# Cross attention with states and a maxout FFN on one core: when three state matrices are transposed and placed, and when x is loaded

## The chip, the core and the metric

The kernel runs on one core of one Trainium2 chip. The metric is the device time of one execution in microseconds (us). Five engines work beside each other and meet through semaphores: TensorE (PE in the profile; its weight loads are PEld), VectorE (DVE), ScalarE (ACT), GpSimd (POOL) and SyncE (SP). SP only issues DMAs here. DMAs issued by GpSimd run on queue 0 of the profile ("software"), those of SP on queue 1, those of ACT on queue 10 (both "hardware"); all of them use the same 16 DMA engines.

## What is computed

There are 8 batches b of 8 heads h. x[b, h] is 512 x 64, state[b, h] is 32 x 64. The weights are 512 x 768 (three) and 768 x 512.

```
scores = x @ state.T / 8                 # 512 x 32 per head
a      = softmax(scores)
xread  = a @ state                       # 512 x 64
a2     = softmax(state @ x.T / 8)        # 32 x 512
sread  = a2 @ x                          # 32 x 64
t      = concat([xread, sread], axis=2)  # 544 rows per head; heads side by side: 8*544 x 512
h      = max(t @ w1, t @ w2, t @ w3)     # x 768
out    = h @ w_out                       # 4352 x 512, float32
```

## The kernel before

All matmuls are in bf16. The kernel never forms xread: it multiplies each head's state with the weights once a batch (G = state @ W, by `g_piece`, `g_cols`) and then multiplies the softmax a with G (`x_maxout`). So for each batch b it needs

- `xT[b]`, x transposed. Batches 0 to 2 transpose on TensorE (`x_transpose`), batches 3 to 7 by a DMA from SP (`x_transpose_dma`, L196), into three buffers in turn;
- `bds[k]` for the pair of batches 2k and 2k+1: the transposed states of each pair of heads as a block diagonal, zero elsewhere. It is made in four steps: `load_st(k)` loads `st_f[k]` (128 KB), `states_cast(k)` makes a bf16 copy `st[k]`, twice side by side (L136), `states_transpose(k)` transposes it into `stT[k]`, on TensorE into PSUM or by a DMA from SP (L154, L158), and `states_place(k)` copies the two halves of 64 partitions into the block diagonal (L163, two instructions);
- `scores(b)`: TensorE multiplies xT[b] with bds (L210), ACT takes the exponential into e (L215);
- `softmax(b)`: VectorE sums and inverts into rden (L223, L225), GpSimd multiplies e by it into a (L230, 1.91 us);
- `aT[b]`, a transposed: on TensorE for b up to 2 (`a_transpose`), by a DMA from SP after that (`a_transpose_dma`, L246);
- `x_pad(b)`: GpSimd copies x[b] into one of two buffers xp with columns of ones between the heads (L256, 1.88 us); `sread(b)` multiplies e with it on TensorE (L277), and its result goes through a small DMA transpose into `ats` (L289, `late_transposes`), read only by the last round;
- `x_maxout(b, m)` for the six column blocks m of 128: six matmuls (L383), ACT copies one product (L387), VectorE takes the two maxima (L390, L391);
- `ffn_out(b, j)` for four row blocks j: six matmuls (L421), ACT copies into `osb[b]` (L424), and at j = 2 and j = 3 GpSimd stores half a batch each (L435), 512 KB.

The order of the instructions on every engine is the order in which the program issues them; nothing is reordered. A written-out prologue handles batches 0, 1 and the front part of 2. Then a loop over b = 2 to 7 runs `x_maxout(b, m)` for m = 0 to 5 and, behind each, the functions of a list `slots[m]`: the scores, softmax, padding and transposes of batch n = b + 1, the G of both, and `ffn_out(b - 1)`. What one engine must wait for holds up all that was issued behind it on that engine. GpSimd's queue therefore mixes arithmetic (a, x_pad, states_cast, states_place) with the issue of loads and stores; SP's queue holds all DMA transposes in order.

The lines around the change, in order of issue: in the prologue `load_st(1, nc.gpsimd)` and `load_x(2)` (L470), `wout`, `load_st(2)`, `load_st(3)`, `load_x(3)`, `load_x(4)`, the memsets of xp and bds on GpSimd; then, later in the prologue, the three `states_cast`, `x_pad(2)`, and `states(1, act)`, which transposes st[1] on TensorE into a PSUM tile of the tag "two" (made by `spare`) and places it by ACT. Scores and softmax of batch 2 follow, `x_transpose_dma(3)`, the DMA transposes of st[2] and st[3], `load_x(5)`, and `states_place` of both on GpSimd. In the loop, `load_x(n + 3)` is in slot 0.

Of the kernel before, what the change touches and what calls it, by code (L numbers as in the profile page):

```python
# [8 lines left out]
F32 = mybir.dt.float32  # L9
# [6 lines left out]
def kernel(  # L16
# [40 lines left out]
    def load_st(k, eng):  # L57
        eng.dma_start(
            out=st_f[k],
            in_=state[2 * k:2 * k + 2].rearrange("b h n d -> (b h n) d").rearrange("(p t) d -> p t d", t=4))  # L60
# [8 lines left out]
    def load_x(b):  # L69
        nc.gpsimd.dma_start(  # L70
            out=x_sb[b][:, 0:XW].rearrange("p (h jd) -> p h jd", h=H),
            in_=x[b].rearrange("h (p j) d -> p h (j d)", j=J))
# [51 lines left out]
    def keep_busy(n):  # L124
        p = pp.tile([128, 1024], F32, tag="two", name="idle")
        for _ in range(n):
            nc.tensor.matmul(p[:, 0:512], zero[:, 0:128], zero, start=True, stop=True)  # L127
# [9 lines left out]

    stT = {}

    def spare(shape):  # L140
        t = pp.tile([128, 2048], BF16, tag="two", name="spare")
        n = 1
        for d in shape[1:]:
            n *= d
        t = t[:, 0:n]
        if len(shape) == 3:
            return t.rearrange("p (a b) -> p a b", a=shape[1])
        return t.rearrange("p (a b c) -> p a b c", a=shape[1], b=shape[2])

    def states_transpose(k, dma):  # L150

        if dma:
            stT[k] = data.tile([128, 4, 128], BF16, name=f"stT{k}")
            nc.sync.dma_start_transpose(out=stT[k], in_=st[k].rearrange("p t c d -> p (t c d)"))  # L154
        else:
            stT[k] = pp.tile([128, 4, 128], BF16, tag="pw", bufs=4, name="pt") if k == 0 else spare([128, 4, 128])
            for t in range(4):
                nc.tensor.transpose(stT[k][:, t, :], st[k][:, t].rearrange("p c d -> p (c d)"), ident)  # L158

    def states_place(k, copy):  # L160
        for c in range(2):
            r = slice(64 * c, 64 * c + 64)
            copy(out=bds[k][r, :, :, c, :].rearrange("p b h (q t) -> p (b h) q t", t=4),  # L163
                 in_=stT[k][r].rearrange("p t (k q) -> p k q t", q=8))

    def states(k, copy):
        states_transpose(k, False)
        states_place(k, copy)
# [7 lines left out]
    def x_transpose(b, g, *copies):  # L176

        if g == 0:
            new(xT, b, [128, H, 2, 128], "xT", bufs=3)
        n = HS // len(copies)  # L180
        for k, copy in enumerate(copies):
            if (b, g) == (2, 0):
                p = spare([128, n, 2, 128])
            else:
                p = pp.tile([128, n, 2, 128], BF16, tag="pw", bufs=4, name="pxt")
            for s in range(n):
                for jj in range(2):
                    nc.tensor.transpose(  # L188
                        p[:, s, jj, :],
                        xv[b][:, 2 * (n * k + s) + g, 2 * jj:2 * jj + 2, :].rearrange("p j d -> p (j d)"),  # L190
                        ident)
            copy(out=xT[b].rearrange("p (s g) j t -> p g s j t", g=2)[:, g, n * k:n * k + n], in_=p)  # L192

    def x_transpose_dma(b):
        new(xT, b, [128, H, 2, 128], "xT", bufs=3)
        nc.sync.dma_start_transpose(out=xT[b].rearrange("p h j t -> p (h j) t"), in_=x_sb[b][:, 0:XW])  # L196
# [131 lines left out]
    def g_cols(b, ms, copies=(act, act), defer=(False, False)):  # L328
        flush_copies()
        for m, copy, wait in zip(ms, copies, defer):  # L330
            if m == 0:
                new(G, b, [128, 2, NM * 384], "G", bufs=3)
            p = pp.tile([128, 2, 512], F32, tag="two", name="pg")
            pv = p[:, :, 0:384].rearrange("p g (i f) -> p g i f", i=3)
            for s in range(HS):
                for g in range(2):
                    nc.tensor.matmul(  # L337
                        pv[32 * s:32 * s + 32, g], bd(b, 2 * s + g)[64 * g:64 * g + 64, g, :],
                        m_cols(w_sb, m)[64 * g:64 * g + 64, s],
                        start=True, stop=True, tile_position=(64 * g, 32 * s))  # L340

            def place(m=m, pv=pv, copy=copy):
                copy(out=m_cols(G[b], m), in_=pv)  # L343

            if wait:
                copies_due.append(place)
            else:
                place()
# [54 lines left out]

    def ffn_out(b, j, split=False):
        if j == 0:
            osb[b] = work.tile([128, J, d_model], F32, tag="osb", name="osb")
        rows = None if b == "s" else out[b * SP:b * SP + S, :].rearrange("(p j) f -> p j f", j=J)
        if split:
            for k, (copy, eng) in enumerate(((dve, nc.sync), (act, nc.scalar))):
                f = slice(256 * k, 256 * k + 256)  # L410
                p = pp.tile([128, 256], F32, tag="pw", bufs=4, name="ph")
                for m in range(NM):
                    nc.tensor.matmul(p, ht[b][:, m, j * 128:(j + 1) * 128], wout_sb[:, m, f],  # L413
                                     start=(m == 0), stop=(m == NM - 1))
                oh = work.tile([128, 256], F32, tag=f"oh{k}", bufs=1, name="oh")
                copy(out=oh, in_=p)
                eng.dma_start(out=rows[:, j, f], in_=oh)
            return
        p = pp.tile([128, d_model], F32, tag="pw", bufs=4, name="po")
        for m in range(NM):  # L420
            nc.tensor.matmul(p, ht[b][:, m, j * 128:(j + 1) * 128], wout_sb[:, m, :],  # L421
                             start=(m == 0), stop=(m == NM - 1))
        o = osb[b]
        act(out=o[:, j, :], in_=p)  # L424
        if b == "s":
            for k in range(4 * j, 4 * j + 4):
                r0 = k * SP + S
                (nc.sync if k % 4 < 2 else nc.gpsimd).dma_start(
                    out=out[r0:r0 + Ns, :], in_=o[32 * (k % 4):32 * (k % 4) + 32, j, :])
            return  # L430
        if b == B - 1 and (j == 1 or j == 2):
            nc.sync.dma_start(out=rows[:, j - j % 2:j + 1, :], in_=o[:, j - j % 2:j + 1, :])
        elif b < B - 1 and j >= 2:
            j0 = 2 * j - 4
            nc.gpsimd.dma_start(out=rows[:, j0:j0 + 2, :], in_=o[:, j0:j0 + 2, :])  # L435
# [19 lines left out]
    load_w(3, (0,))  # L455
    keep_busy(2)
    x_transpose(1, 0, act)
    keep_busy(8)
    g_cols_fast(0, 0)
    a_transpose(0, 0, act)  # L460
# [6 lines left out]
    scores(1, 1, 2)  # L467
    softmax(1, 1, 2, (nc.gpsimd.tensor_mul, J))
    load_w(3, (2,))
    load_st(1, nc.gpsimd)  # L470
    load_x(2)
    nc.gpsimd.dma_start(out=wout_sb, in_=moe_w_out.rearrange("(kk p) f -> p kk f", p=128))
    for k in range(2, B // 2):
# [4 lines left out]
        nc.gpsimd.memset(t.rearrange("p (k c) -> p k c", c=PW)[:, :, 0:2], 1.0)  # L478
    for k in range(1, B // 2):
        nc.gpsimd.memset(bds[k], 0.0)  # L480
    g_cols(0, (1,))
    g_cols(1, (0,))
    sread(0)
# [10 lines left out]
    x_maxout(0, 3)  # L494
    g_cols(0, (4, 5), defer=(False, True))
    x_maxout(1, 2)
    for k in range(1, B // 2):
        states_cast(k, pool)
    x_pad(2)
    x_maxout(0, 4)  # L500
    states(1, act)
    x_transpose(2, 0, dve)
    x_maxout(0, 5)
    g_cols(1, (4, 5), defer=(False, True))
# [2 lines left out]
    scores(2, 0, 2)  # L507
    softmax(2, 0, 2, (nc.gpsimd.tensor_mul, J))
    x_transpose_dma(3)
    for k in range(2, B // 2):  # L510
        states_transpose(k, True)
    late_transposes()
    ffn_out(0, 0)
    x_maxout(1, 4)
    ffn_out(0, 1)
    load_x(5)
    sread(2)
    g_front(2)
    for k in range(2, B // 2):
        states_place(k, pool)  # L520
    x_maxout(1, 5)
    a_transpose(2, 0, act)
    a_transpose(2, 1, dve)
# [6 lines left out]
    for b in range(2, B):  # L530
        n = b + 1
        slots = [[] for _ in range(NM)]
        if n < B:
            slots[0].append(lambda: scores(n, 0, 2))
            slots[1].append(lambda: softmax(n, 0, 2, (nc.gpsimd.tensor_mul, J)))
            slots[1].append(lambda: x_pad(n))
            slots[2].append(lambda: a_transpose_dma(n))
            if n + 2 < B:
                slots[2].append(lambda: x_transpose_dma(n + 2))
            slots[5].append(late_transposes)  # L540
            if n + 3 < B:
                slots[0].append(lambda: load_x(n + 3))
        else:
            for m in range(NM):
                slots[m].append(lambda m=m: s_maxout(m))
        slots[1].append(lambda: g_back(b))
        if n < B:
            slots[4].append(lambda: sread(n))
            slots[4].append(lambda: g_front(n))
        for j, m in enumerate((1, 2, 4, 5)):  # L550
            slots[m].insert(0 if m > 2 else len(slots[m]), lambda j=j: ffn_out(b - 1, j))
        for m in range(NM):
            x_maxout(b, m)
            for f in slots[m]:
                f()
# [36 lines left out]
```

## Time and profile before

| what | value |
|---|---|
| median of 8 runs | 156.45 us (154.94 to 162.09) |
| the profiled execution's own time | 156.33 us |
| its span, first to last instruction | 154.4 us |
| mean granted TensorE clock | 0.996 |
| busy: PE, DVE, ACT, POOL | 146.4, 97.4, 94.9, 64.8 us |
| DMA: moved, mean rate over the span | 21.72 MB, 141 GB/s |

The span is what the trace covers; the execution's own time has 1.93 us more around it. Busy times are unions of an engine's instructions. A row of the page's groups names the line, the engine, the operation, what it writes and reads, and behind the bars its busy time, the mean ns of one, and the idle time of the engine just before these instructions with what ended it. A row of the timeline has start, duration, engine, line, operation and in brackets the idle time before it and what ended that.

### The profile page before, as it was taken

The page shows a single profiled execution, that of the slowest core. Times are in us where ns is not written, and L with a number is a line of the kernel's source. Part 1 is how long each engine was busy: PE and PEld are TensorE (multiplying, and loading weights), DVE is VectorE, ACT ScalarE, POOL GpSimd, SP SyncE. Part 2 cuts the span into 40 slices and gives each one's busy share as a digit, 9 for nine tenths or more (in the row PEclk, how much of TensorE's full clock was granted, in tenths as well). Part 3 has the DMA queues.
Part 4 walks back from the last instruction along what each step waited for, and adds up shares of the span by engine and source line. Part 5 has one row for each costly group of instructions (what it writes and reads, how often), then busy time and mean ns, then how long its engine had stood idle before and what let it go on. Part 6 is the DMA issues. An engine that isn't in the chain of part 4 may idle for free.

```text
span 154.4 us, 3500 instructions
## 1 busy us (share of the span) xinstructions
PE 146.4 (95%) x1390; PEld 71.7 (46%) x1390; DVE 97.4 (63%) x177; ACT 94.9 (61%) x147; POOL 64.8 (42%) x79
## 2 busy tenths in 40 slices
PE   6999999999999967999999999999999999999990
PEld 2555433554444433444444453445344556665450
DVE  3478867869538653768576857785768583565110
ACT  3667688895768446674777477656865637333340
POOL 8997899065229953055106410741073100100050
PEclk9999999999999999999999999999999999999998
DMA  4999999998997799959990883060306030110374
GB/s 110 206 183 190 196 180 162 232 201 122 122 179 134 250 169 154 190 166 235 139 216 6 164 188 136 2 202 15 136 4 204 16 133 0 66 72 0 140 239 169
DMA packets 36736, 21.72 MB, mean 141 GB/s; under 512 B 21968, under 2 KB 34384, under 8 KB 36720
## 3 DMA queue, kind: packets, MB, share of 16 engines
q0 software_dynamic: 17232, 15.08, 53.3%
q1 hardware_dynamic: 19344, 6.29, 22.9%
q8 instruction: 11, 0.18, 0.5%
q10 hardware_dynamic: 144, 0.13, 0.2%
q14 instruction: 5, 0.04, 0.1%
HBM read 15.20 MB, written 8.91 MB: 156 GB/s over the span
## 4 chain that ended last, share of the span: by engine, by line
PE 78%; DMA 9%; POOL 4%; ACT 4%; SPq 1%; issue 1%; DVE 0%
PE pw L383 39%; PE po L421 23%; DMA stT<-st 5%; PE idle L127 4%; DMA aT<-a 4%; PE pg L311 3%; POOL a L230 2%; PE ps L210 2%; ACT G L343 1%; PE pxt L188 1%; PE psr L277 1%; PE pg L337 1%; POOL bd L163 1%; PE psh L210 1%; PE ph L413 1%
## 5 line engine op out<-in xcount | busy, mean ns | idle before, releaser
L383 PE MATMUL pw<-aT,G 128*128 128x512 bf16 x288 | 69.0, 379 | 1.2 <-DMA aT<-a 0.9
L390 DVE TENSOR_TENSOR t<-t,pw 128x512 bf16<-128x512 bf16 (+1 forms) x54 | 35.1, 650 | 30.5 <-ACT t L387 30.4
L421 PE MATMUL po<-wout,ht 128*128 128x512 bf16 x198 | 47.4, 379 | 0.2 <-DVE t L390 0.2
L383 PEld LDWEIGHTS <-G 128*128 128x128 bf16 x288 | 26.7, 98 | 33.2 <-issue 2.7
L391 DVE TENSOR_TENSOR ht<-t,pw 128x512 bf16<-128x512 bf16 (+1 forms) x54 | 35.6, 658 | 5.6
L424 ACT COPY osb<-po 128x512 f32<-128x512 f32 x33 | 19.3, 585 | 29.6 <-PE po L421 29.6
L387 ACT CAST t<-pw 128x512 bf16<-128x512 f32 (+1 forms) x54 | 30.5, 566 | 10.1 <-PE pw L383 9.3
L421 PEld LDWEIGHTS <-ht 128*128 128x128 bf16 x198 | 18.8, 98 | 23.8 <-issue 2.8
L318 ACT CAST G<-pg 128x1024 bf16<-128x1024 f32 x24 | 24.5, 1022 | 3.6 <-PE pg L311 3.2
L435 POOL DMA_DIRECT2D out_dram<-osb x14 | 7.8, 561 | 44.3 <-ACT osb L424 35.7
L230 POOL TENSOR_TENSOR a<-e,rden 128x1024 bf16<-128x1024 bf16 (+2 forms) x10 | 15.2, 1527 | 23.9 <-PE pw L383 15.4
L256 POOL COPY xp<-x 128x2048 bf16<-128x2048 bf16 x6 | 11.3, 1882 | 0.0
L223 DVE TENSOR_REDUCE den<-e 128x32 f32<-128x1024 bf16 (+1 forms) x10 | 9.9, 995 | 0.8 <-ACT e L215 0.7
L343 ACT CAST G<-pg 128x768 bf16<-128x768 f32 x11 | 8.7, 811 | 1.4 <-PE pg L337 1.4
L109 POOL DMA_DIRECT2D w<-in_moe_w_dram x12 | 9.2, 783 | 0.1
L383 PE MATMUL pw<-ats,w 128*128 128x256 bf16 x72 | 8.8, 273 | 0.0
L215 ACT ACTIVATE e<-ps 128x1024 bf16<-128x1024 f32 x6 | 6.2, 1031 | 3.7 <-PE ps L210 3.7
L127 PE MATMUL idle<-zero 128*128 128x512 bf16 x20 | 7.1, 505 | 1.2 <-DVE zero L85 1.2
L383 PEld LDWEIGHTS <-w 128*128 128x128 bf16 x72 | 7.0, 98 | 2.1
L311 PE MATMUL pg<-w,bd 64*32 64x512 bf16 x192 | 7.5, 381 | 0.0
L163 POOL COPY bd<-stT 64x512 bf16<-64x512 bf16 x4 | 4.3, 1072 | 6.2 <-DMA stT<-st 6.0
L210 PEld LDWEIGHTS <-xT 128*128 128x128 bf16 x128 | 5.0, 98 | 2.2 <-ACT xT L192 0.3
(63 smaller groups left out, 87.9 us busy)
## 6 DMA issues: line engine op xcount, KB each, us to landing
out_dram<-osb POOLq DMA_DIRECT2D x14, 512.0 KB, 4.1
x<-in_x_dram POOLq DMA_DIRECT2D x6, 512.0 KB, 9.9
w<-in_moe_w_dram POOLq DMA_DIRECT2D x6, 256.0 KB, 6.2
x<-in_x_dram POOLq DMA_DIRECT2D x3, 256.0 KB, 6.0
w<-in_moe_w_dram POOLq DMA_DIRECT2D x6, 128.0 KB, 6.1
wout<-in_moe_w_out_dram POOLq DMA_DIRECT2D x1, 768.0 KB, 11.8
x0f<-in_x_dram SPq DMA_DIRECT2D x1, 512.0 KB, 3.9
out_dram<-osb SPq DMA_DIRECT2D x1, 512.0 KB, 2.6
```

The source lines that it names most:

```text
L127: nc.tensor.matmul(p[:, 0:512], zero[:, 0:128], zero, start=True, stop=True)
L230: mul(out=a[b][:, r, g0:g1].rearrange("p j g s n -> p j (g s) n"), in0=e[b][:, r, g0:g1].rearrange("p j g s n -> p j (g s) n"), in1=rden[: ...
L256: nc.gpsimd.tensor_copy(out=x_pads[b % 2][:, 2:2 + 2 * H * PW].rearrange("p (k c) -> p k c", c=PW)[:, :, 0:2 * D], in_=x_sb[b][:, 0:XW].re ...
L311: nc.tensor.matmul(ps[g][32 * s:32 * s + 32], bd(b, 2 * s + g)[64 * g:64 * g + 64, g, :], w_sb[64 * g:64 * g + 64, s, c0:c1], start=True, ...
L318: copy(out=G[b][:, :, c0:c1], in_=p[:, :, 0:n])
L343: copy(out=m_cols(G[b], m), in_=pv)
L383: nc.tensor.matmul(p[:, 0:n], lhs(i, k), rhs(k), start=(k == 0), stop=(k == nk - 1))
L387: nc.scalar.copy(out=t0[:, 0:n], in_=pw[0][:, 0:n])
L390: nc.vector.tensor_max(t1[:, 0:n], t0[:, 0:n], pw[1][:, 0:n])
L391: nc.vector.tensor_max(ht[b][:, m, :], t1[:, 0:n], pw[2][:, 0:n])
L421: nc.tensor.matmul(p, ht[b][:, m, j * 128:(j + 1) * 128], wout_sb[:, m, :], start=(m == 0), stop=(m == NM - 1))
L424: act(out=o[:, j, :], in_=p)
```

## The change

- `load_st(1)` is issued from ACT's queue after the copy of xT of batch 1, instead of from GpSimd after the weights; at its old place on GpSimd stands `states_cast(1)`, and SP transposes st[1] by a DMA then. `states_place(1)` is done by GpSimd behind the memsets of bds. The transposes on TensorE and the copies on ACT for k = 1 are gone, and with them `spare`; its second user, `x_transpose(2, 0)`, takes its PSUM tile directly.
- st[2] is still transposed ahead of the loop, st[3] in round b = 2 of the loop, behind the transpose of x[5]. `states_place(2)` and `states_place(3)` are issued in slot 3 of rounds b = 2 and 3.
- `load_x(5)` moves from ahead of the loop into slot 0 of round 2, and x[6] and x[7] follow one round later than before.
- `osb` has three buffers instead of two. The lines that store are not touched: each batch is stored in two halves before and after.

```diff
-    def spare(shape):
-        t = pp.tile([128, 2048], BF16, tag="two", name="spare")
...
-            stT[k] = pp.tile([128, 4, 128], BF16, tag="pw", bufs=4, name="pt") if k == 0 else spare([128, 4, 128])
+            stT[k] = pp.tile([128, 4, 128], BF16, tag="pw", bufs=4, name="pt")
...
-                p = spare([128, n, 2, 128])
+                p = pp.tile([128, 2 * n, 2, 128], BF16, tag="two", name="spare")[:, 0:n]
...
-            osb[b] = work.tile([128, J, d_model], F32, tag="osb", name="osb")
+            osb[b] = work.tile([128, J, d_model], F32, tag="osb", bufs=3, name="osb")
...
     x_transpose(1, 0, act)
+    load_st(1, nc.scalar)
     keep_busy(8)
...
     load_w(3, (2,))
-    load_st(1, nc.gpsimd)
+    states_cast(1, pool)
+    states_transpose(1, True)
     load_x(2)
...
     for k in range(1, B // 2):
         nc.gpsimd.memset(bds[k], 0.0)
+    states_place(1, pool)
...
-    for k in range(1, B // 2):
+    for k in range(2, B // 2):
         states_cast(k, pool)
     x_pad(2)
     x_maxout(0, 4)
-    states(1, act)
     x_transpose(2, 0, dve)
...
     x_transpose_dma(3)
-    for k in range(2, B // 2):
-        states_transpose(k, True)
+    states_transpose(2, True)
     late_transposes()
     ffn_out(0, 0)
     x_maxout(1, 4)
     ffn_out(0, 1)
-    load_x(5)
     sread(2)
     g_front(2)
-    for k in range(2, B // 2):
-        states_place(k, pool)
...
             if n + 2 < B:
                 slots[2].append(lambda: x_transpose_dma(n + 2))
+                slots[0].append(lambda: load_x(n + 2))
+            if b == 2:
+                slots[2].append(lambda: states_transpose(3, True))
             slots[5].append(late_transposes)
-            if n + 3 < B:
-                slots[0].append(lambda: load_x(n + 3))
+            if b < 4:
+                slots[3].append(lambda: states_place(b, pool))
```

More of the change, by code (lines that the diff above doesn't have):

```diff
@@ L138 @@
     stT = {}
-    def spare(shape):
-        t = pp.tile([128, 2048], BF16, tag="two", name="spare")
[L142 to L148, printed above, removed]
     def states_transpose(k, dma):
```

## The prediction, made before the changed kernel was run

> **What bounds the kernel now.** I read the page's busy shares first, then who made TensorE wait, then the order of time on TensorE and GpSimd around those waits, then the DMA issues. (Old line numbers throughout; the new file's are ten lower.)
>
> ```profile
> PE 146.4 (95%) x1390; PEld 71.7 (46%) x1390; DVE 97.4 (63%) x177; ACT 94.9 (61%) x147; POOL 64.8 (42%) x79
> ```
>
> TensorE (PE) is busy 146.4 of 154.4 us and no other engine is above 63%. Of its 8.0 us of idle time, 1.2 lie ahead of the first matmul and 3.7 behind the last (the chain ends with ACT at 150.75). The rest is in this view of TensorE's waits:
>
> ```profile
> PE psr L277 <- POOL xp L256: 1.2, 1, 1.2
> PE pw L383 <- DMA aT<-a: 0.9, 1, 0.9
> PE pw L383 <- ACT G L343: 0.3, 1, 0.3
> PE pg L337 <- ACT G L343: 0.3, 1, 0.3
> PE po L421 <- DVE t L390: 0.2, 1, 0.2
> ```
>
> The first two are what a change can win, and both happen once. TensorE's timeline shows their full price. These are the score matmuls of batches 3, 4 and 5, each issued at the same point of the loop over b:
>
> ```profile
> 44.27 0.63 PE L210 MATMUL ps<-bd,xT 128*128 128x64 bf16 x16
> ...
> 55.80 0.43 PE L277 MATMUL psr<-xp,e 128*32 128x65 bf16 x32 [1.18 <-POOL xp L256]
> ...
> 60.45 1.45 PE L383 MATMUL pw<-aT,G 128*128 128x512 bf16 x6 [0.85 <-DMA aT<-a]
> 61.74 0.63 PE L210 MATMUL ps<-bd,xT 128*128 128x64 bf16 x16
> ...
> 76.95 0.63 PE L210 MATMUL ps<-bd,xT 128*128 128x64 bf16 x16
> ```
>
> A round takes 61.74 to 76.95 = 15.21 us, and the first round, with the same work on TensorE, 44.27 to 61.74 = 17.47 us. So the two waits cost **2.26 us**; the idle column says 2.03, because a matmul's end lies after the next one's start. Why the first round is late stands in GpSimd's timeline:
>
> ```profile
> 36.70 1.91 POOL L230 TENSOR_TENSOR a<-e,rden 128x1024 bf16<-128x1024 bf16 x1 [1.64 <-DVE rden L225]
> 38.56 0.95 POOL L70 DMA_DIRECT2D x<-in_x_dram  x1
> 45.55 4.45 POOL L163 COPY bd<-stT 64x512 bf16<-64x512 bf16 x4 [6.04 <-DMA stT<-st]
> 49.94 1.10 POOL L435 DMA_DIRECT2D out_dram<-osb  x2
> 51.03 0.92 POOL L70 DMA_DIRECT2D x<-in_x_dram  x1
> 52.01 1.91 POOL L230 TENSOR_TENSOR a<-e,rden 128x1024 bf16<-128x1024 bf16 x1
> 53.87 1.88 POOL L256 COPY xp<-x 128x2048 bf16<-128x2048 bf16 x1
> ```
>
> GpSimd waits 6.04 us for the transposed states, places four halves, then issues two stores and a load that piled up behind, and only at 52.01 does the softmax product a of batch 3, although its input rden was there at 49.47 (VectorE's timeline: 49.12 + 0.35). a is then transposed by a DMA (issue 53.95, landing 6.4 later), and x_pad(3) ends at 55.75, where sread(3) on TensorE wanted it at 54.5.
>
> **The loop: states of k = 2 and 3 placed later, loads moved.** In the new order GpSimd has, after a(2) (ends 38.6): store 1 of batch 0 (its data are there at 37.96), store 2 (ACT's last osb copy ends 43.76, so 43.8 to 44.3), the load of x5 (0.95, to 45.3), and then it is free for a(3) at 49.5. With the durations of the rows:
> - a(3) 49.5 to 51.4, x_pad(3) to 53.3. sread(3) wants it at 54.5: 1.2 us of room, the first wait goes.
> - aT(3) is issued at 51.4. Its five issues landed after 3.1 (least) to 6.4 (most), so 54.5 to 57.8. x_maxout(3,0) wants it at 60.45 less both waits, about 58.1. The second wait goes too; what is late next has 0.3 to 3.6 us of room. I expect a landing after under 4 us, because the two stores and a load that filled the DMA engines from 50 on are now issued from 38.6 to 45.3.
> - states_place(2) comes behind x_pad(3): two copies of 1.07, 53.3 to 55.5; scores(4) wants it at 59.5. Behind it queue batch 1's stores and the load of x6, which nobody needs soon. states_place(3) follows x_pad(4) in the same way, two rounds ahead of scores(6).
> - Loads one batch later: x5 from 38.56 to 44.3, x6 from 51.0 to about 58.5, x7 from 61.0 to about 75. Landing took 7.1 to 15.4 us. On SP's queue xT(5), xT(6), xT(7) wait for them, at worst some 2 to 6 us, and behind these stand only the third state transpose, an ats transpose (read at the end) and the next round's aT, over 7 us later. xT itself is read a round and more after it. Cost nothing; without that cover it would be the next aT, late by what the load is late.
> - The third osb buffer frees nothing: no store or osb copy in the waits had waited for a buffer (ACT's osb copies waited for PE po alone). The stores were two a batch already and the diff leaves them so. Nothing.
>
> Sum of this part: **-2.26**.
>
> **The start: states of k = 1.** Off TensorE go four transposes (28.56 to 28.79, **-0.22**), off ACT two copies (29.04 to 30.2), behind which no PE wait stands. On come:
> - The load of st_f[1] on ACT's queue, at about 10.1. Its issue (0.37 in the one ACT row of that kind, L417) fits in the 1.03 us that ACT idles there ahead of pgf. But its 128 KB share the DMA engines with the weights: at the 193 GB/s of 4 to 35 us that is 0.7 us, or 0.5 at the 247 of 2.0 to 4.5. The third weight load of chunk 1 lands at 14.03 (7.69 + 6.34), and g_cols(0, 1) reads it at 14.07: no room. It would start up to 0.6 late, but ACT's copy behind it waits anyway for an exp that ends at 14.71, and the next fixed point (a_transpose(1, 1), 17.77) has 0.1 spare. So 0 to 0.3; I take **+0.1**. The Trainium skill speaks against this edit: DMA: Bandwidth & Descriptors, section Rules for kernel authors, says that spreading DMAs over SP, ACT and GpSimd brings no bandwidth and saves only issue time. By the rule alone the weights pay the full transfer, +0.6; by the rows the exp hides most of it. On GpSimd the freed issue (0.56) is replaced by states_cast(1) (0.68), so x2's load moves by 0.1.
> - The DMA transpose of st[1]: cast at 18.5 to 19.2, SP issue at 19.2. states_place(1) stands on GpSimd behind the memsets, which end at 26.5, and takes 2.15; scores(2) reads bds[1] at 32.6. So it is free if it lands by 30.4, that is within 11.2 us. The two stT transposes of before took 6.5 and 7.6, the second partly beside a load: landing about 26.8. Behind the place stand states_cast(2) (waits until 32.0 for its load anyway), x_pad(2) and a(2). Free.
> - The same transpose delays queue 0. Beside one of 516 packets queue 0 moved 810 in 3.0 us (41.5 to 44.5), where alone it moved 777 in 2.0 (69.2 to 71.2): 0.9 us lost. x2 lands at 27.86, TensorE would read it at 28.1. stf1 no longer stands in the queue ahead of x2, which gives some back. 0 to 0.7, I take **+0.2**. Weights of w_out (31.65, wanted at 33.1), x3 and xT(3) (landed 41.08, wanted at 44.1, now beside store 1 of batch 0, which moves 512 KB in 3.1 when alone) keep room, in the worst case a few tenths.
>
> **Sum**: -2.26 - 0.22 + 0.1 + 0.2 = -2.2. The profiled execution took 156.33 us (1.93 more than its span), the median of the eight is 156.45, so the sum stands for both: **154.2 us**, -1.4%. About 1% is what a measurement of this kernel can tell from no change.
>
> **Rivals.**
> 1. *The gain is partly paid back at the start or at xT(3)* : x2 0.7 late, chunk 1 costs 0.3, xT(3) a few tenths. For it: the DMA share is 9 tenths in nearly every slice up to 38 us, and x2 has only 0.5 us of room. Against: ACT and VectorE have slack there. -2.5 + 0.7 + 0.3 + 0.3 = -1.2: 155.2.
> 2. *Nothing shows*: aT(3) lands as late as before, because other transfers (xT(4), x5) take the place of the stores, or the edits that cost nothing take 2 us somewhere unseen. For it: in 54 to 57 us queue 1, which carries the transposes, moved no packet at all beside queue 0. Against: at 51.4 queue 0 should be empty. About 156.2.
> 3. *The first state transpose starves (slower)*. Place: stT1 issued at 19.2, with queue 0 full until x4 lands at 38.06 (22.70 + 15.4). GpSimd then sits at states_place(1), and scores(2) on TensorE waits. It decides from a landing after 30.4, cancels the whole gain at about 32.6, and each us more is one us. Here again row and rule part. The row:
>
> ```profile
> q0 software_dynamic: 747, 0.47, 117.5%
> ```
>
> This is the whole list of queues that moved anything in 54 to 57, with aT(3) issued at 53.95. Taken as a law it puts stT1 behind x4: landing near 38, place to 40.2, scores(2) 7.6 late: 156.3 - 2.2 + 7.6 = 162. The rule (DMA: Bandwidth & Descriptors, section Queues, rings and completion order: each DMA engine takes turns between the queues with work, a packet at a time) gives it its turn, and the 41.5 to 44.5 row shows that: 516 packets through in 3.0 us beside a load of x, so landing near 25, and 154.2. I side with the rule, since the row of the load of x is the nearer one, but keep the other end.
>
> **Chances.** Forecast 58% (own range 153.5 to 154.8); rival 1 17%; rival 2 10%; rival 3 12%, from 157 to 162; 3% for a larger gain. Faster by over 1% takes nearly all of the forecast, the larger gain and little of rival 1: 0.60. Within 1%: the rest of these and rival 2, 0.28. Slower by over 1%: rival 3, 0.12. The range takes in rivals 1 and 2 and leaves rival 3 out: 153.3 to 156.5.
>
> **What would show it.** Right: rounds from scores(3) to scores(4) of 15.2 us; no wait of psr for xp or of pw for aT; a(3) on GpSimd waiting for rden, not behind places; bd copies near 26.5, 53 and 69; PE busy near 146.2 in a span near 152.3. Wrong: a wait of GpSimd's bd copy for stT past 30 us with PE idle ahead of ps near 32.5 (rival 3); PE waiting at the transposes of x2 near 28.3 or for chunk 1 near 14 (rival 1); aT(3) landing after 58 (rival 2).

## The result, and the profile after

The changed kernel took 154.45 us (median of 11 runs), the kernel before 157.1 (median of 32). The ratio is **0.990, with an interval of 0.986 to 0.993**. It counts, of each kernel, only runs within 1.5% of its fastest; this leaves out many long runs of the kernel before. Ten of the changed kernel's runs lie from 154.1 to 154.6, those of the kernel before from 154.5 to 163.9. One run of each stands far off (172.4 and 839.5), and neither is explained. The profiled execution took 154.10 us, forecast 154.2; its span is 152.2 against 154.4.

The page's busy shares, the answer to the first line shown of before (line numbers are now ten lower):

```profile
PE 146.0 (96%) x1386; PEld 71.5 (47%) x1386; DVE 97.2 (64%) x177; ACT 93.8 (62%) x145; POOL 66.4 (44%) x80
```

TensorE's idle time is 6.2 us instead of 8.0. Here is who made it wait (engine, line, releaser: us, times, longest):

```profile
PE idle L127 <- DVE zero L85: 1.2, 1, 1.2
PE pg L327 <- DMA w<-in_moe_w_dram: 0.4, 1, 0.4
PE pg L327 <- ACT G L333: 0.3, 1, 0.3
PE pw L373 <- ACT G L333: 0.2, 1, 0.2
PE po L411 <- DVE t L380: 0.2, 1, 0.2
```

The waits for xp and for aT are gone; one of 0.4 for the weights of chunk 1 is new. TensorE's timeline at the same places as before:

```profile
44.28 0.63 PE L200 MATMUL ps<-bd,xT 128*128 128x64 bf16 x16
...
54.57 0.43 PE L267 MATMUL psr<-xp,e 128*32 128x65 bf16 x32
...
58.20 1.46 PE L373 MATMUL pw<-aT,G 128*128 128x512 bf16 x6
59.49 0.63 PE L200 MATMUL ps<-bd,xT 128*128 128x64 bf16 x16
...
74.70 0.63 PE L200 MATMUL ps<-bd,xT 128*128 128x64 bf16 x16
```

The first round of the loop now takes 59.49 - 44.28 = 15.21 us, like the second. Up to 44.28 nothing was won or lost (44.27 before). So all 2.2 us come from the first round, and GpSimd's timeline shows how:

```profile
26.68 2.20 POOL L153 COPY bd<-stT 64x512 bf16<-64x512 bf16 x2
...
44.61 0.92 POOL L70 DMA_DIRECT2D x<-in_x_dram  x1
49.69 1.91 POOL L220 TENSOR_TENSOR a<-e,rden 128x1024 bf16<-128x1024 bf16 x1 [4.16 <-DVE rden L215]
51.55 1.88 POOL L246 COPY xp<-x 128x2048 bf16<-128x2048 bf16 x1
53.38 2.22 POOL L153 COPY bd<-stT 64x512 bf16<-64x512 bf16 x2
```

a(3) waits for its input rden and for nothing else; x_pad(3) is done at 53.4, and the places follow where nobody waits for them.

### The profile page after: what moved, and what is told of

Its sections match the earlier page's. It is cut to its first block, busy times and chain, and to the rows that moved or that the text cites. A ratio compares the mean times of both kernels' runs of the same rounds, so it can differ in the third digit from the quotient of the medians.

```text
span 152.2 us, 3495 instructions
## 1 busy us (share of the span) xinstructions
PE 146.0 (96%) x1386; PEld 71.5 (47%) x1386; DVE 97.2 (64%) x177; ACT 93.8 (62%) x145; POOL 66.4 (44%) x80
## 4 chain that ended last, share of the span: by engine, by line
PE 85%; DMA 4%; POOL 4%; ACT 2%; issue 1%; DVE 0%; POOLq 0%
PE pw L373 44%; PE po L411 29%; DMA w<-in_moe_w_dram 4%; PE pg L301 4%; POOL w L109 2%; PE ps L200 2%; PE psr L267 2%; PE pg L327 2%; POOL x L80 2%; ACT G L333 1%; PE ph L403 1%; ACT t L377 1%; DVE t L380 0%; PE pat L231 0%; PE pxt L178 0%
## 5 line engine op out<-in xcount | busy, mean ns | idle before, releaser
L380 DVE TENSOR_TENSOR t<-t,pw 128x512 bf16<-128x512 bf16 (+1 forms) x54 | 35.1, 650 | 29.7 <-ACT t L377 29.6
L373 PEld LDWEIGHTS <-G 128*128 128x128 bf16 x288 | 26.8, 98 | 32.0 <-issue 2.7
L414 ACT COPY osb<-po 128x512 f32<-128x512 f32 x33 | 19.3, 585 | 29.6 <-PE po L411 29.6
L308 ACT CAST G<-pg 128x1024 bf16<-128x1024 f32 x24 | 24.5, 1022 | 2.3 <-PE pg L301 1.8
L153 POOL COPY bd<-stT 64x512 bf16<-64x512 bf16 x6 | 6.5, 1077 | 0.3
```

Source lines behind the costliest of these rows:

```text
L308: copy(out=G[b][:, :, c0:c1], in_=p[:, :, 0:n])
L373: nc.tensor.matmul(p[:, 0:n], lhs(i, k), rhs(k), start=(k == 0), stop=(k == nk - 1))
L380: nc.vector.tensor_max(t1[:, 0:n], t0[:, 0:n], pw[1][:, 0:n])
```

## The experiments

Two theories were open after the result. **A**: the order on GpSimd alone made a(3), and with it aT(3), late. **C**: the DMA engines were too full behind a(3), and what cures that is the later loads. Runs 1 to 4 were taken together, as were 5 to 8 and 9 to 12; each is compared with the runs of the kernel before in its own group. Lines left out of an edit are marked by three dots.

**1. The changed kernel again.** No edit.

> The changed kernel once more, beside its parts on one chip. Theory A (GpSimd's order in the first round of the loop): no wait of sread(3) for xp and of x_maxout(3, 0) for aT, span 152.2, time 154.4, in every run nearly the same. Any rival expects the same here; the run is the measure for the three others.

Measured: 154.1 us, six runs from 153.6 to 154.7, ratio 0.987 (0.982 to 0.992). The kernel before ran from 155.2 to 165.9 beside it. The small spread is itself a part of the result.

**2. The loop part alone.** The prologue and `osb` stay as before.

```diff
-    for k in range(2, B // 2):
-        states_transpose(k, True)
+    states_transpose(2, True)
...
-    load_x(5)
-    for k in range(2, B // 2):
-        states_place(k, pool)
...
+            if b == 2:
+                slots[2].append(lambda: states_transpose(3, True))
             slots[5].append(late_transposes)
-            if n + 3 < B:
-                slots[0].append(lambda: load_x(n + 3))
+            if b < 4:
+                slots[3].append(lambda: states_place(b, pool))
+            if n + 2 < B:
+                slots[0].append(lambda: load_x(n + 2))
```

> The loop part alone: states 2 and 3 placed in slot 3 of rounds 2 and 3, the transpose of st[3] in round 2, x5 to x7 loaded a round later; states 1 on TensorE and ACT as before, osb with two buffers. Theory A: both waits go, -2.3 us against before, within 0.3 us of the changed kernel, and the spread of the runs shrinks as in the changed kernel. Rival B (the start part brings the gain): within 0.5 us of before, both waits still there.

Measured: 154.39, seven runs from 153.8 to 155.2, ratio 0.988 (0.984 to 0.993), no wait for xp or aT. Its first round takes 59.92 - 44.71 = 15.21 us:

```profile
44.71 0.63 PE L210 MATMUL ps<-bd,xT 128*128 128x64 bf16 x16
...
59.92 0.63 PE L210 MATMUL ps<-bd,xT 128*128 128x64 bf16 x16
```

The loop part is enough for the whole gain and for the small spread.

**3. Only the places moved.** As run 2, with `load_x(5)` and `load_x(n + 3)` as before.

> Only the placing of states 2 and 3 (and the DMA transpose of st[3]) moves into the loop; the loads of x stay where they were, x5 at 38.6 and x6 ahead of a(3). Theory A (GpSimd's order): a(3) starts near 49.5 and both waits go, -2.3 us. Rival C (the DMA engines were too full behind a(3), and the later loads cure that): the wait for xp goes (-1.3), that for aT stays at about 1 us because x6's load still runs beside aT(3): -1.3 in all.

Measured: 156.5, 14 runs from 154.5 to 165.2, ratio 0.994 (0.990 to 0.998). A missed: the order on GpSimd alone brings, by this ratio, about half of the gain, and by the medians (156.5 against 157.0) less. Its profile is of one of the longest runs, 162.16 us. There a(3) starts at 50.0 as hoped and sread no longer waits, but TensorE's timeline has

```profile
63.92 2.29 PE L383 MATMUL pw<-aT,G 128*128 128x512 bf16 x5 [5.22 <-DMA aT<-a]
```

aT(3) was issued at 51.9 and landed 11.9 us later. x6's load, issued at 44.95 ahead of it, landed at 59.0. C was right about where the time stays, though it expected a wait of about 1 us.

**4 and 9. The start part alone**, twice: all edits for the states of k = 1, none of those for k = 2 and 3 or for the loads of x, and two `osb` buffers.

```diff
+    load_st(1, nc.scalar)
...
-    load_st(1, nc.gpsimd)
+    states_cast(1, pool)
+    states_transpose(1, True)
...
+    states_place(1, pool)
...
-    states(1, act)
```

> The start part alone: st_f[1] loaded from ACT's queue, cast early, transposed by a DMA and placed by GpSimd behind the memsets; the loop, its loads and places and the two osb buffers as before. Theory A: -0.2 for the transposes, up to +0.2 for the weights' delay: 0.0, both waits of the first round stay (2.3 us together) and the runs spread as in before. Rival B (the start part brings the gain): -2 us.

> The start part alone a second time, because its runs lay between 153.65 and 161.78. Theory E (without st_f[1] in GpSimd's queue x3 lands 1 to 1.6 us earlier, so xT(3) and both state transposes may get through ahead of the load of x5; where they do, both waits go, and where the second one does not, as in its profile, GpSimd waits for it and aT(3) lands late): runs between 153.7 and 162 again; if the profile falls into a run near 154, both stT land by about 42 and no wait of PE for aT is left. Theory A: about before, 156 to 157, both waits in every run.

Measured: 154.68 (153.65 to 161.78) and 160.73 (154.0 to 163.62), six runs each. The ratio of run 4 was 0.988 (0.982 to 0.995); run 9 has too few runs near its shortest for one. The runs fall apart into four of 153.65 to 154.0, two of 155.5 and 156.0, and six of 159.8 to 163.6. A, which expected 156 to 157, missed. Theory E was half seen: x3 lands earlier (xT(3) is issued at 34.7 in both profiles, 35.8 before), and st[2] is placed by 43.2; but in both profiles, of long runs, st[3]'s transpose went out behind the load of x5 and landed at 48.0 and 48.6. Whether it lands early in the short runs was not seen, since no profile fell into one. So in four of twelve runs the start part alone is as fast as the changed kernel, although the prediction's sum gives it nothing (-0.22 + 0.1 + 0.2); how it gets there stays open. The long runs read as follows (run 9, TensorE's waits):

```profile
PE pw L373 <- DMA aT<-a: 4.9, 1, 4.9
PE idle L127 <- DVE zero L85: 1.2, 1, 1.2
PE psr L267 <- POOL xp L246: 1.0, 1, 1.0
```

and its busy times by stretches (stretch, then PE, PEld, DVE, ACT, POOL busy with counts, granted clock, DMA share, GB/s):

```profile
60.00:64.00 4.00, 0.00 (x0) 0.00 (x0) 0.00 (x0) 0.47 (x1) 1.44 (x2) 1.00 0.90 157
64.00:66.00 2.00, 1.27 (x4) 0.46 (x5) 0.00 (x0) 0.22 (x1) 0.00 (x0) 0.50 1.17 339
66.00:68.00 2.00, 2.00 (x21) 1.06 (x20) 1.19 (x2) 0.36 (x1) 0.00 (x0) 0.64 1.22 257
68.00:70.00 2.00, 2.00 (x23) 0.67 (x23) 0.59 (x2) 1.83 (x3) 0.00 (x0) 1.00 1.95 149
```

TensorE stands still from 60 to 64.7. The granted clock is 0.50 from 64 on, for two us and most of the next two, some 3.4 us in all; TensorE works in the last 2.7 of these. From scores(3) at 44.74 to scores(4) at 67.24 the round takes 22.50 us, 7.3 more than the changed kernel's 15.21. From start to start the wait for xp makes 1.0 of this, that for aT 5.1, and the six matmuls behind it, at half clock, 1.2 (2.51 to the next start instead of 1.29):

```profile
44.74 0.63 PE L200 MATMUL ps<-bd,xT 128*128 128x64 bf16 x16
...
64.73 2.72 PE L373 MATMUL pw<-aT,G 128*128 128x512 bf16 x6 [4.88 <-DMA aT<-a]
67.24 0.72 PE L200 MATMUL ps<-bd,xT 128*128 128x64 bf16 x16
```

The span is 159.8 - 152.2 = 7.6 above the changed kernel's, so the two waits and the clock behind them are nearly all of it.

**5. Only the loads later.** The places stay ahead of a(3).

```diff
-    load_x(5)
...
-            if n + 3 < B:
-                slots[0].append(lambda: load_x(n + 3))
+            if n + 2 < B:
+                slots[0].append(lambda: load_x(n + 2))
```

> Only the loads of x5, x6 and x7 come a round later; states 2 and 3 are placed ahead of a(3) as before. Theory A: GpSimd still waits for the transposed states until about 45.5 (somewhat less, since no load of x5 runs beside the transposes), so the wait for xp stays near 1 us and a(3) near 51 to 52: -0.2 to -0.8. Rival C (full DMA engines were the cause): the transposed states land 2 us sooner, aT(3) lands after 3 us, and most of the 2.3 us go: -1.5 or more.

Measured: 157.33, six runs from 154.3 to 160.1; ratio 0.985 (0.976 to 0.995), which rests on the two shortest runs. In the profile (157.38 us) both transposed states land by 41.8, a(3) starts at 49.3 waiting for rden alone, and the wait for xp is gone: the loads alone clear GpSimd's queue, against A. But the two stores and x5's load now go out at 45.2 to 46.4, right behind the places. x5 lands at 57.0, aT(3) after 9.6 us at 60.8, and TensorE waits 2.9:

```profile
60.95 1.46 PE L383 MATMUL pw<-aT,G 128*128 128x512 bf16 x6 [2.92 <-DMA aT<-a]
```

Neither half keeps aT(3) clear; C's "after 3 us" missed too.

**6. The transpose of st[1] later.** In the changed kernel, cast and transpose go behind the memsets, directly ahead of `states_place(1)`.

> The changed kernel with the cast and the DMA transpose of st[1] moved behind GpSimd's memsets, so that the transpose is issued at about 27.3 instead of 19.2. Theory D (the start is free only as long as the transposed states land by 30.4, then each us costs one): landing after the same 7.4 us at 34.7, places until 36.9, scores(2) on TensorE about 4.0 us late, time about 158.4. Rival: the slack elsewhere swallows it, under +1.5 us.

Measured: 158.55 (157.1 to 161.6, 15 runs), ratio 1.009 (1.005 to 1.013) to the kernel before. The transpose was issued at 26.8 and landed after 7.4 us. GpSimd's place waits for it (timeline), and TensorE for the place (waits):

```profile
34.34 2.14 POOL L153 COPY bd<-stT 64x512 bf16<-64x512 bf16 x2 [7.58 <-DMA stT<-st]
```

```profile
PE ps L200 <- POOL bd L153: 3.3, 1, 3.3
```

D holds. The profiled span is 156.0, 3.8 above the changed kernel's, and 34.34 + 2.14 = 36.48 is just ahead of the start of scores(2), 36.54, against 32.84 in the changed kernel. The slack in front of scores(2) was real and ends where the prediction put it.

**7. The load of st_f[1] later.** `load_st(1, nc.scalar)` moves from behind `x_transpose(1, 0, act)` to behind `load_w(3, (2,))`.

> The changed kernel with the load of st_f[1] issued from ACT's queue behind the exp of scores(1, 1), at about 14.2 instead of 9.2, when the weights of chunk 1 have landed. Theory: TensorE's wait of 0.4 for the weights at 14.1 goes, but a_transpose(1, 1) near 17.8 is set by GpSimd's product a, so at most 0.1 us is won: same. Rival (that wait is paid in full): -0.4 us.

Measured: 154.28 (153.7 to 155.0, six runs), ratio 0.983 (0.977 to 0.989) in a group in which the changed kernel itself was not run. The wait for the weights is gone from the profile and the time is the changed kernel's. As expected.

**8. Two osb buffers.** `bufs=3` taken out of the changed kernel.

> The changed kernel with two osb buffers instead of three. Theory: no osb copy waits for a store, so nothing changes: within 0.2 us of the changed kernel. Rival: with the places ahead of the stores of batch 1, the copy of batch 3's first block waits for batch 1's store (landing near 63) and TensorE behind it: up to +1 us.

Measured: 154.12, four runs from 154.1 to 154.8, the ratio of run 7 (0.983). ACT's osb copies wait for PE po alone (29.6 us in 32 waits, longest 1.7), as with three buffers. The third buffer does nothing.

**10. x5 early, x6 and x7 late.** Runs 3 and 5 left a third theory, F: aT(3) is late when a load of x is in flight as it is issued. In the changed kernel, `load_x(5)` goes back ahead of `sread(2)`.

> The changed kernel with only x5's load back at its old place, ahead of batch 0's stores; x6 and x7 stay a round later. Theory F (what makes aT(3) late is a load of x in flight when it is issued at 51.6): x5 has landed by then, aT(3) lands after 3 to 4 us, no wait: within 0.3 us of the changed kernel, runs close together. Rival (a load beside xT(3) and the state transpose delays all transposes on SP's queue): aT(3) late, +1 us and runs spread.

Measured: 154.25, 22 runs from 153.85 to 154.8. aT(3) lands after 3.7 us. F holds here: where x5 is loaded does not matter. As worded, F says too much: in the changed kernel x5's load, too, is in flight as aT(3) is issued, but it lands 1.9 us later. It takes a load with longer to go.

**11. x6 ahead of a(3).** In the changed kernel, x6 is loaded right behind x5.

> The changed kernel with x6's load one round earlier, right behind x5's and ahead of a(3), at about 45.5; the places stay in the loop. Theory F: x6 is in flight when aT(3) is issued at 51.6, aT(3) lands near 59 to 61 where TensorE wants it at 58.2: +1 to +3 us, and runs spread as in the run with the places alone. Theory A (GpSimd's order alone): same as the changed kernel.

Measured: 154.65, 22 runs from 153.9 to 162.6. Its ratio is 0.997 (0.992 to 1.003) where run 10, in the same group, has 0.993 (0.989 to 0.997). The intervals overlap, but nine of its 22 runs are over 155 us and none of run 10's 22. In the profile (155.43 us) aT(3) is issued at 52.1, x6 lands at 58.4 and aT(3) 0.9 behind it:

```profile
59.40 1.46 PE L373 MATMUL pw<-aT,G 128*128 128x512 bf16 x6 [0.55 <-DMA aT<-a]
```

F has the mechanism and the direction: moving this one load brings the wait and the long runs back. Its +1 to +3 was too much for the median (+0.4 to run 10).

**12. The kernel before again**, for a second profile.

> The kernel before once more, for a second profile. Theory F: the wait of x_maxout(3, 0) for aT is of another length than the 0.9 us of the first profile, and the time differs by just that: runs of 158 to 160 us would have a wait of 3 to 4 us. Rival (its longer runs come from a lower clock all along or from elsewhere): the wait is about 0.9 whatever the time.

Measured: 157.52 us, with waits of 1.0 for xp and 0.8 for aT. So F's expectation missed: this run is 1.2 us longer than the first profiled one with nearly the same two waits; 0.4 of it is there by the scores of batch 4 (62.12 against 61.74; a wait of 0.5 for the first x lies ahead of them), and the other 0.9 lies behind the last matmul (it ends at 151.10 of a span of 155.7, against 150.71 of 154.4), where the last stores go out. Not every long run is explained by aT(3).

No run points to a version better than the changed kernel: runs 2, 7, 8 and 10 lie within 0.3 us of it.

## Why the prediction was right

- *The two waits of the first round, -2.26.* Right to the hundredth in the profile (17.47 to 15.21 us), and runs 2, 3 and 11 tie it to them. The step "a landing after under 4 us" of aT(3) is what carries it: issued at 51.6, landed after 3.2. The reason given, that two stores and a load are issued earlier, is not enough for it: in run 3 they are too, but there the load is x6's, with x5's ahead of it. That x6 waits a round is half of the change: with the places moved and x6's load still ahead of a(3), the second wait is back, at 5.2 us in run 3 and 0.5 in run 11, against 0.9 before.
- *The loads one batch later, "nothing".* The cost was nothing, but the edit of x6 is a gain. x5's is indeed nothing (run 10).
- *Four transposes off TensorE, -0.22.* Mis-sized: 0.0. TensorE is 0.18 ahead at the transposes of x2 (28.61 against 28.79) and level again at 31.09 (31.07 before). The trace of after has the pg matmuls there start at 30.45, 0.17 ahead of before, but their second half only at 30.80, after VectorE's copy of the spare PSUM tile:

```profile
30.06 0.68 DVE L182 COPY xT<-spare 128x1024 bf16<-128x1024 bf16 x1
```

  Before, the second half started at 30.79. The tag "two" has two tiles, so the second half of g_cols(1, (4, 5)) takes the one that this copy reads, and VectorE makes the copy no earlier than before (30.01). By the trace the saving went into waiting for it; no run tried another tile.
- *x2 late, +0.2.* Mis-sized the other way: x2 landed at 26.90, 0.96 earlier than before. Taking st_f[1] out of queue 0 ahead of x2 outweighed the transpose beside it: x2 lands 8.8 us after its issue in the kernel before, 7.8 in the changed kernel, and 7.7 in run 6, where no transpose runs beside it. TensorE never waited for x2, so this term came to nothing as well. That the two errors cancel in the sum is luck.
- *Chunk 1, +0.1.* TensorE waited 0.42 at 14.5 for a landing at 14.50, and a_transpose(1, 1) started at 17.82 instead of 17.77: 0.05. The weights landed 0.47 later than before (14.03), near the 0.6 that the prediction worked out by the rule of the Trainium skill, and with the load of st_f[1] issued later (run 7) this wait is gone; the exp and GpSimd's a hid all but 0.05. So the rule was right about the transfer, and the rows about what of it TensorE pays.
- *stT1.* Issued at 19.17, landed after 7.37 at 26.54; the memsets end at 26.6. The 26.8 taken from two earlier landings was near. The 25 that rival 3 took from the packets of the 41.5 to 44.5 row was not: that transpose, too, landed only at 47.76, 7.6 after its issue, so packets that are through are not a landing. Rival 3 did not come; run 6 shows what it would have cost.
- *Rival 2's mechanism* (queue 1 held up beside queue 0) was the one at work in the kernel before and in runs 3, 4, 5, 9 and 11, and only the order of the loads kept it out of the changed kernel.

## What to carry to other kernels

When one round of a loop is longer than the next with the same work, the difference between equal points of the two is the price of its waits, better than the idle column. An engine that issues DMAs must be planned twice: what waits behind the instruction, and which transfers are in flight when the next urgent DMA is issued. A load that nobody needs yet goes behind the urgent transfer, even when the queues are different ones. And a median hides what such an edit does for the spread: 153.6 to 155.2 in runs 1, 2, 7, 8 and 10, against 154.1 to 166 for the kernel before in the same three groups.

## What the runs showed of the hardware

**A DMA transpose beside a load lands late.** aT(3) of 256 KB lands after 3.7 us in run 10, with no load in flight, and after 3.2 in the changed kernel, where x5's load lands 1.9 us after the issue. With a load that has longer to go it lands after 6.3 to 6.4 in the two profiles of before, and after 7.1 to 11.9 in runs 3, 4, 5, 9 and 11. In run 11 and in both profiles of before it lands 0.9 to 1.0 us behind the load that was in flight (x6: 58.4, 59.4, 59.7). In runs 3, 4, 5 and 9 it lands 3.2 to 4.8 us behind it, so the load is not all that can hold it. In 4, 5 and 9 a store issued 1.8 us behind the transpose lands within 0.4 us of it; in 3, 5 and 11 xT(4), ahead of it on SP's queue, was still under way as well. No run separates these.

In the changed kernel stT1, issued at 19.17, shows where the time goes. These are the queues that moved anything in 19.2 to 21 us, in 21 to 23, and in 24.5 to 26.5 (packets, MB, and the summed time of the packets as a share of 16 engines, so that it can pass 100%; queue 8, one packet, left out):

```profile
q0 software_dynamic: 692, 0.35, 142.6%
```

```profile
q0 software_dynamic: 315, 0.15, 126.7%
q1 hardware_dynamic: 439, 0.11, 52.3%
```

```profile
q0 software_dynamic: 770, 0.40, 144.7%
q1 hardware_dynamic: 21, 0.00, 1.4%
```

The Trainium skill (DMA: Bandwidth & Descriptors, section Queues, rings and completion order) has each DMA engine take turns between the queues with work, a packet at a time. The middle stretch agrees: most of the transpose's packets go through in it, beside those of the load. The other two show what the turns leave out: for nearly 2 us after the issue none of its packets moves, and the last 21 come only after 24.5. It counts as landed at 26.54, shortly before x2 (26.90). For aT(3) of before, the 54 to 57 us row of the prediction shows the first of these for 3 us; in the changed kernel's last rounds, with nothing else in flight, the packets of an aT start 1.2 us after its issue and it lands after 3.1. What holds the first packets and the last ones was not tried.

**The clock after a pause.** TensorE's pauses of 2.9 (run 5) and 3.3 us (run 6) left the granted clock at full. After 3.9 and 4.9 us (runs 4 and 9) it was half for some 3.4 us, after 5.2 (run 3) for about twice that: mean clocks of 0.989 and 0.979 over spans of 160 us. The Trainium skill (TensorE: Matmul & The Clock Gate, section What's actually happening) has the clock halved after an idle window of about 3.4 us; the runs agree. The kernel before has the same mean clocks in its long runs: in the last group 0.988 or 0.989 in most of those from 158 to 160 us, 0.977 to 0.987 in those above 162. That fits a wait for aT of over 3.4 us in them; no profile of such a run of before was taken.
